# New work lists for the five queues of a sorted-attention and feed-forward kernel, with batch 1's k loaded between the halves of w_in

## The chip, the cores and the metric

The kernel runs on one core of a Trainium2 chip. A core has five instruction queues that run at once: TensorE (PE: matmuls, with the loads of their weights shown as PEld), VectorE (DVE), ScalarE (ACT), GpSimd (POOL) and SyncE (SP), and DMA queues beside them. The metric is device microseconds of one launch; lower is better. All times below are microseconds (us).

## What is computed

Four batches of eight heads, 768 positions and head size 64 go through an attention in which the blocks of k and v are mixed by a matrix that is first balanced by five Sinkhorn rounds; the result is the input of a feed-forward layer. Scale, the subtraction of maxima inside the rounds and the small epsilons are left out here:

```python
P = sort_net                                  # (4, 8, 8, 8)
for _ in range(5):
    P = exp(P - max(P)); P = P / sum(P, -1); P = P / sum(P, -2)
k_sorted = einsum('bhij,bhjcd->bhicd', P, k_blocks)   # 8 blocks of 96 positions
v_sorted = einsum('bhij,bhjcd->bhicd', P, v_blocks)
scores = scale * q_blocks @ k_sorted.T        # block against block, 96 x 96
attn = softmax(scores)
x = (attn @ v_sorted) as (3072 tokens, 512)
h = x @ w_in                                  # (512, 2048)
g = max(h, 0) + alpha * min(h, 0)
out = g @ w_out                               # (2048, 512)
```

## The kernel before

**An order written out by hand.** The body first describes all work as a graph of 1227 numbered operations, each with the engines that may do it, what it reads and writes, and a function that issues its instructions. It then hands `SEQ`, a list of the 1227 numbers, to `G.arrange`. For each engine the operations are issued in the order in which they stand in `SEQ`; a letter behind a number (p, a, d) puts an operation that has a choice on POOL, ACT or DVE, and one without a letter goes to its first engine. `emit` derives the semaphore waits from reads and writes, so any order that `arrange` accepts computes the same. A second table, `WARM`, puts extra matmuls of the identity into PE's queue: `89:14:y` is fourteen of them ahead of operation 89, into the bank `y`. They compute nothing that is used. `BURST` is a count of small matmuls of zeros that PE does first.

**The start (batch 0).** POOL issues the loads: q (op 4), k (5), v (6), batch 1's k (138), w_in in four parts (130 to 133), w_out in two (134, 135), batch 1's v (147, 148) and its q by heads (139 to 146). The Sinkhorn rounds (42 to 78) run on DVE and ACT; a matmul (79) spreads the mixing matrix and DVE makes the block mask BDK (80) from it.

- q is turned in six units: matmuls against the identity (odd ops 81 to 91), each with a copy into QTz on ACT (the even ops behind them, 82 to 92).
- k is mixed and turned in six units (matmuls 93, 95, 98, 100, 102, 104), each with a copy into KT by ACT or DVE (94, 96, 99, 101, 103, 105) and one small copy for a pad of KT (97).
- v is first spread in eight copies (106 to 113, POOL or DVE), then mixed in eight units (matmuls 114 to 128, even), each with a copy into VS by ACT or DVE (115 to 129, odd).

**Attention by groups.** A group is one block of one batch over all eight heads; there are 32, numbered g. For a group PE makes scores (for g = 0 op 149, for g = 1 op 158), DVE their maxima (150, 159), PE the scores once more in the other orientation with the maxima subtracted ("second scores", 151, 160), ACT the exponentials ET (152, 161), PE the product with v (153, 162), DVE the reciprocal of the sums and the scaled result xq (154, 155), PE a transpose (156, 165), and DVE or ACT the copy into xT (157, 166). From batch 1 on, transposes are done by DMAs that SP issues. For g = 2 the scores are 184 and the second scores 186, for g = 3 scores 205, second scores 207, product 209 and transpose 212, for g = 4 scores 238 and second scores 240; these stand among the first feed-forward units.

**Feed-forward.** For two groups at first, later four, sixteen units of w_in: four (or two) matmuls, a relu of the negative on ACT, and a fused multiply and add on DVE that writes hT. The first ones are ops 193 and 196, then 199, 202 and so on. Every 128 tokens follow four quarters against w_out, a copy out of the bank and a store.

**Batches 1 to 3** are prepared between feed-forward units. k and v are spread into zero-padded tiles by POOL or DVE copies ("conv": for batch 1's k ops 247 to 250, 253, 254, 257, 258 and so on; for the first piece of batch 3's v op 713), mixed by PE with the masks BDM and BDV (251 and 255 are the first units of batch 1's k, 252 the copy of the first; the matmuls at line 629 are these units) and copied by ACT or DVE. The masks of batches 1 to 3 come from a second spread (167 to 176). q of batches 1 to 3 is turned by DMA transposes (batch 1's six are 178 to 183); batch 3's v (643 to 646) is loaded when the last q turn of batch 2 (570) has landed. Group 13's scores are op 561, its exponentials 564; op 674 is the feed-forward unit that needs the place they free.

The engines' orders around the change, before, in the numbers above (PE until the first feed-forward, warm-up matmuls as [w]):

```
POOL loads: 4 5 6 138 130 131 132 133 134 147 148 ... 135 ... 139-146
PE: burst [w14] 89 83 81 87 91 85 [w8] 79 [w2] 93 102 [w2] 104 95 100 98 [w9] 114 [w6] 158 118 116 120
    149 124 160 136 122 126 [w4] 128 151 [w1] 162 [w3] 153 177 165 156 184 167 196
```

The rules that fix an operation's engine and a copy's choice are these:

```python
EITHER = ("act", "dve")
SHIFT = ("pool", "dve")
letters = {"p": "pool", "a": "act", "d": "dve"}
e = letters.get(x[-1], op.engs[0])
op.eng, op.pos, op.start = e, len(self.order[e]), float(n)
```

Lines that the profile names: 372 copies by `copy`; 419 and 435 the loads of k and v; 409 the q turns of batches 1 to 3; 539 and 543 the first spread and the mask BDK; 600 the matmuls of `pairs` (q turns and batch 0's k); 629 k of batches 1 to 3; 653 the spread copies of batch 0's v; 669 and 674 the v units; 712, 715, 727, 736 scores; 721 maxima; 759 exponentials; 768 the product with v; 776 and 779 reciprocal and xq; 794 the transpose; 808 warm-up; 823, 833 and 836 the feed-forward's matmuls, relu and fused operation; 862 the second matmuls.

Of the kernel before, what the change touches and what calls it, by code (L numbers as in the profile page):

```python
# [39 lines left out]
155 20 21 165 156 166d 141 184 157a 167 185 140 168 142 169 196 193 186 194 197 195 199 198 187 27 202 170 203 205  # L42
200 204 188 201 214 206 220 215 217 189 218 207 221 219 222 226 216 229 190 227 223 230 273 228 224 171 208 231 225
235 191 236 238 192a 237 232 239 261 313p 251 262 209 233 347p 252a 240 210 263 139 211 255 241 270 234 403 212 264
404 256a 213d 291 301d 271 242 258p 175 259 292 257p 274 260a 352p 265 272 267 311p 243 266 279 244 300p 293 280
268 312p 281 282 269 310p 294 245 174 285 304d 351p 246d 275 286 283 348p 287 284 338 305p 302 339 295 303a 314 288
296 315 306 289 316 340 307a 290 176 297 320 178 341 317 276 318 321 319 179 298 322 379 299a 308 380 323 309a 342
326 324 343 349 344 327 381 350a 325 328 345 353 382 346d 329 354d 332 180 330 572p 383 333 331 357 277a 402 334
335 384 361 360p 385 183 336 373 362 574p 337 358a 363 391p 419 359d 386 355p 364 420 367 573p 365 374 368 366 182
421 356d 388 387d 370 389d 395p 375 577p 369 371 392 390p 435 372 393a 429 394p 436 396 430 376 397d 422 437 445p  # L50
431 432 578p 377d 398 446p 181 453 399d 447p 405 454 449p 438 433 455 465 448p 400 434 459 401a 466 456 460 451 461
457 406 467 452d 483 458 415 423 450d 477 462 478a 475p 468 172 424 413 495 476d 463 407 425 484 378 418 496 408
411 464 481 482a 409d 412 486 485 426 479p 549 487 427d 497 480p 488 439 506p 507 440 492 508d 509p 489 414 441 493
498 511 494 505p 490 442 525 443a 491 510p 516 278 512a 417 526 513 517 535p 537 518 514 469 550 571p 527 515 416
470 519 471 536p 522 538d 520 528 472 561 523 521 539 473a 562 543 540a 499 524 544 541 428 551 500 563 501 546
542d 534 502 545 575 503a 597 576d 547 555 474 548 529 556 606 530 558 607a 612p 557 564 552 609p 531 559 608p 560
610 553a 444 579 613d 638p 611a 598 582 580 532 635 583 637d 591 581 599 636d 585 570 584 592 586 533a 639 600 587
588 640a 626 589 614 627 641 615 565 590 646 593 628 566 644 616 617 643 642d 620 645 567 618 629 594 621 619 622
677 595a 568 504 623 678 569a 659 624 601 410 660 662 602 679 603 554 663 625 661 604 668 605a 718p 680 704 669
713p 671 705 714p 664 672 706 673 665 670 630 719 631 674 666a 632 752p 707 648 686 675 649 633 676 692 687 667  # L60
748p 634a 716d 596 720a 739 688 650 681 689 749d 715p 717d 698 647 690 658 750 691 699 693 751a 700 652 701 173 740
778p 721 702 682 753p 694 703 722 741 723 695 754 724 755d 696a 742 727 683 725 854p 779 726 728 733 777p 729 812p
768 848d 730 654 769 756 731 655 780a 708 732 734 757 709 657 782d 770 783 758 735 813p 784d 651 762 710 771 759
849p 763 656 743 764 760 814 736 847p 711 815a 761 850p 781d 803 744 853p 737d 785 653 684 804 765 786 788 766 805
767 789 787 794 745 797 806 838 798 816 839 772 817a 790 795 799 818 697 840 791 773 796 738 774 820 746 819d 800
792a 775 807 801 851 826 821 802 852a 793 822 873 823 841 874 832 824 881 833 827 747 888p 882a 834 875 828 825 846
808 855 884d 809 885 835 856 883d 685 911p 886a 857 842 887p 836 829 912p 837 712 909 843 830a 861 858 862 910a 901
863 867 859 831 860 889 902 876 913 864 890 891 868 811 865 844 903 869 914d 866 895 915 904 892 896 897 870 893
810 916a 894 877 871a 917 935 776 918 898 936 920 899 919 937 921 900 878 879 929 926 880 961 927 905 962 930 922
938 928 981 963 931 923 906 845 907 932 943 964 933 987 934 944 982 924d 908 988 939 946 945 983 989 940 941 949  # L70
955 947 990 965 948 956 950 1007 958 1008 951 959 1009 960 952 957 972 966 967 969 1010 973 984 974 970 953a 971
872 1033 985a 978 925 1034 975 979 991 980 976 1018 1035 992 977 998 1019 999 1036 995 1000 1020 996 942 997 1004
993 1059 1005 968 1001 1060 1021 1002 1061 954 1003 1047 1006 1011 1015 1024 1016 1048 1017 1025 1012 1026 1085
1027 1022d 1013 1030 1023 1028 1079 1031 1014 1032 1080 1029 994 1044 1086 1041 1045 1062 1081 1046 1042 1087 1043
1049 986 1053 1037 1054 1056 1055 1050 1057 1058 1067 1051d 1105 1068 1038 1070 1039 1116 1071 1040 1072 1117 1069
1088 1076 1106 1073 1077 1063 1078 1074 1082 1075 1096 1064 1083a 1065 1093 1097 1118 1098 1094 1107 1095 1119 1102
# [203 lines left out]
def bass_sinkhorn_attn__then__act_prelu_kernel(  # L280
# [749 lines left out]
```

## Time and profile before

| | us |
|---|---|
| time, median of 3 runs | 238.87 (238.43 to 239.08) |
| the profiled execution's own time | 238.79 |
| its span in the trace | 237.1 |
| PE busy | 228.4 (2511 matmul rows) |
| PE loading weights, beside it | 143.5 |
| DVE busy | 169.4 |
| ACT busy | 151.9 |
| POOL busy | 74.1 |

The profile is of one execution. Its span begins with the first instruction and is 1.7 us shorter than the time of that execution. A row of the timeline has the start, the duration, the engine, the line of the kernel, what is written from what, the shape, how many instructions, and in brackets the idle time before it with what ended it. PE is the engine with the most work; its warm-up matmuls count as busy too, so its share does not say by itself how much of it the computation needs.

### The profile page before, as it was taken

What the parts mean: (1) busy time and instruction counts of PE and PEld (TensorE: products, weight loads), DVE (VectorE), ACT (ScalarE), POOL (GpSimd) and SP (SyncE); (2) the same over time, 40 slices, a digit from 0 to 9 for tenths busy, and PEclk for the clock granted to TensorE, in tenths of its full rate; (3) what the DMA queues carried; (4) which work ended last, traced back from release to release, by engine and by line L of the source; (5) the groups of instructions that cost most, each with busy time, mean ns of one, the idle gap of its engine ahead of it and who ended that gap; (6) DMA issues with size and microseconds to landing.
All of it is one profiled execution on the core that took longest, in us unless ns stands there. A gap on an engine that the chain in (4) does not pass through costs nothing.

```text
span 237.1 us, 6254 instructions
## 1 busy us (share of the span) xinstructions
PE 228.4 (96%) x2511; PEld 143.5 (61%) x2540; DVE 169.4 (71%) x353; ACT 151.9 (64%) x423; POOL 74.1 (31%) x140
## 2 busy tenths in 40 slices
PE   7798999999999999999999999999999999999995
PEld 3455678788666666666566665655655555555544
DVE  4745788889999997878887667676766587744350
ACT  4463356677886988886678786756863646353332
POOL 7959812905759521238292020000000000000000
PEclk9999999999999999999999999999999999999999
DMA  5999999999999998999999795542442423600033
GB/s 93 211 215 170 209 219 200 177 210 156 191 93 150 148 129 176 155 181 179 141 100 131 188 179 119 99 91 48 124 100 74 97 50 82 136 0 0 4 133 133
DMA packets 71453, 31.36 MB, mean 132 GB/s; under 512 B 64504, under 2 KB 65280, under 8 KB 71424
## 3 DMA queue, kind: packets, MB, share of 16 engines
q0 software_dynamic: 22896, 13.63, 44.0%
q1 hardware_dynamic: 48528, 17.33, 38.6%
q8 instruction: 20, 0.33, 0.6%
q14 instruction: 9, 0.07, 0.1%
HBM read 27.28 MB, written 6.29 MB: 142 GB/s over the span
## 4 chain that ended last, share of the span: by engine, by line
PE 90%; DMA 3%; DVE 3%; issue 1%; ACT 1%; POOLq 0%
PE psH L823 34%; PE psYP L862 29%; PE psS L862 4%; PE psS L712 3%; DMA hT<-in_q_dram 3%; PE psO L768 3%; PE psYP L808 3%; PE psYP L669 2%; PE psYP L629 2%; PE psS L727 2%; PE psO L794 1%; PE psS L736 1%; PE psS L715 1%; PE psO L862 1%; DVE hT L836 1%
## 5 line engine op out<-in xcount | busy, mean ns | idle before, releaser
L836 DVE SCALAR_TENSOR_TENSOR hT<-t,omaT,psH 128x384 bf16<-128x384 f32 (+1 forms) x139 | 77.3, 570 | 36.2 <-ACT t L833 34.8
L823 PE MATMUL psH<-xT,w_in_bf 128*128 128x384 bf16 (+1 forms) x556 | 96.9, 311 | 0.1
L833 ACT ACTIVATE t<-psH 128x384 f32<-128x384 f32 (+1 forms) x139 | 63.2, 462 | 49.5 <-PE psH L823 48.2
L862 PE MATMUL psYP<-w_out_bf,hT 128*128 128x512 bf16 x308 | 77.6, 379 | 1.5
L823 PEld LDWEIGHTS psH<-xT,w_in_bf 128*128 128x128 bf16 x556 | 49.5, 98 | 29.1 <-DVE hT L836 1.9
L862 PEld LDWEIGHTS psYP<-w_out_bf,hT 128*128 128x128 bf16 x336 | 30.9, 98 | 28.2
L748 ACT ACTIVATE Esb<-psS,nf 96x96 bf16<-96x96 f32 x192 | 46.3, 346 | 2.0 <-DVE nf L721 2.0
L721 DVE TENSOR_REDUCE nf<-psS 96x8 f32<-96x768 f32 x24 | 22.8, 950 | 6.5 <-PE psS L712 6.0
L658 POOL COPY VDz<-VST 64x192 f32<-64x192 f32 x39 | 20.5, 525 | 20.2 <-DMA VST<-in_v_dram 16.5
L779 DVE TENSOR_TENSOR xq<-psO,rec 96x512 bf16<-96x512 f32 x31 | 21.2, 683 | 0.5
L616 POOL COPY KSz<-KS 64x256 f32<-64x256 f32 x28 | 11.5, 412 | 32.1 <-PE psYP L629 18.8
L401 POOL DMA_DIRECT2D QN<-in_q_dram x24 | 20.0, 839 | 3.3 <-DMA QTz<-QN 2.7
L712 PEld LDWEIGHTS psS<-KT,QTz 128*96 128x96 bf16 x192 | 12.1, 124 | 3.3
L808 PE MATMUL psYP<-identb 128*128 128x512 bf16 x48 | 13.6, 419 | 0.4 <-ACT identb L372 0.4
L372 ACT ACTIVATE VS<-psYP 112x512 bf16<-112x512 f32 x15 | 10.3, 686 | 5.4 <-PE psYP L674 3.2
L768 PEld LDWEIGHTS psO<-VS,ET 112*128 112x128 bf16 x248 | 11.1, 98 | 3.6 <-ACT ET L759 0.2
L768 PE MATMUL psO<-VS,ET 112*128 112x65 bf16 x248 | 12.7, 194 | 0.0
L712 PE MATMUL psS<-KT,QTz 128*96 128x96 bf16 x192 | 12.6, 208 | 0.0
L372 ACT ACTIVATE KT<-psYP 128x512 bf16<-128x512 f32 x15 | 9.0, 599 | 2.6 <-PE psYP L629 1.6
L372 ACT ACTIVATE outstg<-psYP 128x512 f32<-128x512 f32 x13 | 7.7, 604 | 3.2 <-PE psYP L862 3.2
L669 PEld LDWEIGHTS psYP<-BDV,VDz 128*128 128x128 bf16 x192 | 8.2, 98 | 2.3 <-ACT VS L372 0.2
L669 PE MATMUL psYP<-BDV,VDz 128*128 128x64 bf16 x192 | 9.5, 193 | 0.0
(137 smaller groups left out, 200.2 us busy)
## 6 DMA issues: line engine op xcount, KB each, us to landing
out_dram<-outstg SPq DMA_DIRECT2D x23, 256.0 KB, 2.5
KS<-in_k_dram POOLq DMA_DIRECT2D x3, 768.0 KB, 13.6
QN<-in_q_dram POOLq DMA_DIRECT2D x24, 96.0 KB, 5.4
w_in_bf<-in_moe_w_in_dram POOLq DMA_DIRECT2D x4, 512.0 KB, 17.0
w_out_bf<-in_moe_w_out_dram POOLq DMA_DIRECT2D x2, 1024.0 KB, 23.6
VST<-in_v_dram POOLq DMA_DIRECT2D x4, 384.0 KB, 17.9
hT<-in_q_dram POOLq DMA_DIRECT2D x1, 768.0 KB, 7.8
VST<-in_v_dram POOLq DMA_DIRECT2D x1, 768.0 KB, 11.0
```

The costliest lines, as they stand in the source:

```text
L372: return e.activation(o, i, ACTF.Copy) if e is nc.scalar else e.tensor_copy(o, i)
L669: inst = e.matmul(AP(t, off + dd * 64, [[row, 128], [1, 64]]), AP(VDz, (u % VSL * 4 + dd // 2) * 256 + dd % 2, [[VSL * 1024, 128], [2, 128]]),
L712: inst = e.matmul(o, AP(QTz[n], hp * 3072 + h4 * 768 + i * 96, [[6144, 128], [1, 96]]), AP(KT[n], (h4 * 8 + i) * bk, [[ld, 128], [64, 2], ...
L721: G.add(DVE, lambda e: e.tensor_reduce(AP(nx, 0, [[8, 96], [4, 2], [1, 4]]), AP(psX, 0, [[1024, 96], [512, 2], [96, 4], [1, 96]]), AxisLis ...
L748: inst = e.activation(AP(Esb[me], p * 128, [[1024, 96], [64, 2], [1, 48]]), AP(psX, (p // 4) * 512 + (p % 4) * 96, [[1024, 96], [48, 2], [ ...
L768: inst = e.matmul(AP(psZ, hp * 512 + h4 * 68, [[1024, 128], [1, 65]]), AP(ET[me] if far else ET[m], pos(h4, hp) * 96, [[800, nk], [1, 128] ...
L779: G.add(DVE, lambda e: e.tensor_tensor(out=AP(xq[me], 0, [[512, 96], [256, 2], [64, 4], [1, 64]]), in0=AP(psZ, 0, [[1024, 96], [512, 2], [ ...
L808: inst = e.matmul(AP(bank[0], bank[1], [[1024, 128], [1, 512]]), identb[:, :], AP(identb, 0, [[128, 128], [0, 4], [1, 128]]))
L823: inst = e.matmul(AP(pt, poff, [[1024, 128], [1, n]]), AP(w_in_bf, kt * DFF + ft // 2 * 256 + ft % 2, [[KT_TILES * DFF, 128], [2, 128]]), ...
L833: G.add(ACT, lambda e: e.activation(AP(t1[tb], 0, [[384, 128], [1, n]]), AP(pt, poff, [[1024, 128], [1, n]]), ACTF.Relu, scale=-1.0), t_ac ...
L836: G.add(DVE, lambda e: e.scalar_tensor_tensor(out=AP(hT, ft * RING + tok % RING, [[FT_TILES * RING, 128], [1, n]]), in0=AP(t1[tb], 0, [[38 ...
L862: inst = e.matmul(AP(bank[0], bank[1], [[1024, 128], [1, n]]), AP(hT, ft * RING + tok % RING, [[FT_TILES * RING, 128], [1, 128]]), AP(w_ou ...
```

## The change

Three tables change and nothing else: `BURST`, `WARM` and `SEQ`. The first eight entries of the list of operations differ little; from the ninth on all five queues have another order. The count of operations is the same, 1227. 84 of them change their engine: copies that spread v of batches 1 to 3 (13 from POOL to DVE, 7 back), copies that spread k (9 from POOL to DVE, 5 back), the copies behind v units (10 from DVE to ACT, 9 back) and k units (5 and 2), the copies out of the last feed-forward bank (7 from DVE to ACT, 5 back), the xT copies (5 and 5) and two small ones (the clearing of VD0 and KT's pad, from POOL to DVE). DVE has 365 operations instead of 353, POOL 124 instead of 136, ACT 254 as before.

The warm-up table goes from 11 entries with 51 matmuls to 10 with 39, and the burst from 130 to 122 matmuls. The diff, with the long list cut to the part around the start:

```diff
-BURST = 130
+BURST = 122
 WARM = """
-89:14:y 79:8:y 93:2:y 104:2:y 114:9:y 158:6:y 153:3:h 205:1:y 207:1:y 128:4:y 162:1:y
+91:10:y 79:7:y 102:2:y 104:2:y 118:6:y 116:9:y 153:2:h 167:1:p 214:1:y 207:1:y
 """
 SEQ = """
-0 7 11 2 3 1 4 8 42 9 22 28 43 14 44 45 46 47 19 18 48 5 49 50 15 51 39 52 53 6 54 55 25 56 138 57 58 29 23 59 60
-12p 61 62 130 63 64 31 65 32 66 13 37 89 67 68 83 69 81 84 70 87 71 91 131 88 10 85 132 72 40 73 90 133 74 75 86
-134 76 41 77 82 78 26 79 92 147 80 148 93 102 94d 103a 104 95 105a 100 98 99a 38 109d 106p 35 111d 36 96a 108p 112d
-16 34 101a 33 114 107p 115d 97p 146 158 118 159 110p 116 119a 120 250p 149 121d 124 248p 160 117d 125a 113p 30 135
-136 161 122 137 150 249p 126 254p 127a 123d 24 128 144 151 129d 143 247d 17 152 162 145 163 164 153 177 253p 154
...
+0 7 11 2 27 3 10 1 4 42 43 8 9 91 28 44 40 45 46 47 48 49 50 51 52 53 54 55 56 57 39 81 85 87 89 83 5 24 20 6 130
+26 131 138 132 133 134 147 25 13 23 148 146 135 19 16 58 59 60 61 62 63 64 65 66 67 86 68 69 70 71 72 29 37 82 38
+73 74 35 75 76 77 78 79 80 102 93 103d 94a 84 88 14 247p 253p 250p 21 144 143 249p 145 141 140 15 254p 31 248p 98
+12d 104 95 100 41 108d 111d 34 17 110d 92 99a 105a 90 96a 109d 97d 101d 118 113d 112d 107d 106d 116 114 158 119d
+149 124 159 115a 120 150 121d 160 125a 117a 122 136 123d 161 126 128 129a 151 152 36 137 127d 33 162 163 164 153
...
```

In the new order POOL's loads are 4, 5, 6, 130, 131, 138, 132, 133, 134, 147, 148, 146, 135, then 144, 143, 145, 141, 140 with copies of batch 1's k between them (247, 253, 250 ahead of 144). PE's start reads: burst, [w10], 91 81 85 87 89 83, [w7] 79, [w2] 102 93 98, [w2] 104 95 100, [w6] 118, [w9] 116 114 158 149 124 120 160 122 136 126 128 151 162, [w2] 153 177 165 184 156, [w1] 167 193 196.

More of the change, by code (lines that the diff above doesn't have):

```diff
@@ L45 @@
[L45 to L64, printed above, removed]
@@ new lines @@
+229 239 236 230 240 225 237 210 231 232 241 211 251 261 252d 273 262 233 263 212 291 213a 234 292 255 270 256a 264
+242 259 293 271 265 260a 294 272 173 266 243 244 279 313p 257p 258p 301p 30 310p 300p 311p 351p 267 282 268 274 280
+269 283 302 281 284 338 303a 245 285 339 305p 22 142 139 32 403 348p 347p 352p 312p 246a 288 306 286 295 289 304d
+287 290 296 297 340 307a 314 315 317 275 308 318 341 316 319 320 323 321 298 324 309d 379 349 322 299a 325 326 350a
+380 329 342 327 353 330 178 381 354a 343 328 332 357 179 333 331 335 344 358d 276 345 388 336 382 337 180 364 334
@@ new lines @@
+389d 419 359p 356p 390p 355p 404 394p 402 360p 391p 346a 365 277a 361 392 383 362 420 366 384 385 363 373 370 374
+421 393d 371 372 386 367 422 387a 368 435 396 432 397a 369 433 429 430 375 436 437 434 18 398 456 395d 431 399d 457
+458 453 400 376 454 450p 446p 578d 462 465 447p 577p 449p 448p 455 172 445d 466 377a 401a 463 459 460 405 423 451
+406 464 461 424 452d 425 467 181 183 278 438 182 468 378 483 495 477 496 486 426 484 478a 427d 485 487 497 407 481
+439 489 488 492 490 475p 574p 506p 505p 479p 510p 476p 440 571d 441 572p 415 413 418 480p 408 442 525 491 493 482a
@@ new lines @@
+443a 409a 494 526 513 469 514 470 471 507 516 549 515 508d 472 519 527 517 498 528 511 520 550 512a 473d 499 518
+522 523 521 500 501 176 524 537 538a 561 543 502 562 411 535p 412 536p 509p 414 417 416 544 503a 545 539 546 547
+563 551 529 555 564 556 548 530 531 540d 573d 558 557 559 560 552 597 541 532 579 553a 542a 582 580 533d 598 581
+583 428 570 599 591 575 565 585 584 588 566 576d 606 608d 592 593 626 600 589 607a 610 567 590 586 613d 609d 587
+611a 646 612p 644 637p 643 645 617 618 627 638d 614 615 619 568 594 635 628 569d 616 601 623 620 595d 602 636d 662
@@ new lines @@
+765 735 814 815d 762 766 763 767 764 803 736 794 737a 785 795 786 804 816 788 796 743 800 787 817d 744 745 805 789
+797 838 771 684 711 801 798 818 772 819a 802 849d 823 790 839 840 847p 854d 791 773 799 848d 851 774 792a 820 873
+824 826 821 852a 853d 874 825 822 875 746 806 775 841 876 697 827 881 807 882a 808 809 828 832 835 885 842 829 833
+834 836 837 830d 653 884p 685 712 747 888p 887p 912p 883p 911p 886a 855 843 844 856 909 858 901 867 910a 859 857
+860 902 913 861 862 914d 864 868 915 863 916d 903 865 877 889 890 869 935 870 891 878 866 871a 936 895 892 896 893
@@ new lines @@
+904 738 937 897 894 879 880 810 938 793 920 921 917 898 961 905 922 923 899 918 900 919 906 962 907 926 929 924a
+927 930 963 908 845 964 776 811 831 872 949 981 928 931 939 943 932 944 945 987 940 950 955 933 934 956 946 947 982
+951 988 957 941 989 969 948 970 971 958 1007 952 975 965 959 960 972 1008 953a 976 973 974 977 966 983 1018 978 995
+1009 1033 984 979 996 985a 980 998 999 1034 997 1019 1001 1000 967 1035 1004 990 942 991 1047 1020 1002 1003 1015
+1059 1010 954 846 925 1005 1006 992 993 1024 1011 1021 1048 1016 1025 1060 1017 1026 1022d 1012 1013 1061 1030 1036
@@ new lines @@
+968 1023 986 1014 994 1062 1027 1031 1032 1079 1085 1044 1028 1029 1045 1041 1049 1080 1086 1042 1046 1056 1087
+1043 1057 1058 1053 1054 1050 1037 1055 1038 1039 1051a 1070 1067 1105 1081 1071 1072 1076 1068 1069 1077 1073 1063
+1116 1106 1078 1096 1074 1064 1075 1065 1097 1098 1093 1088 1082 1089 1102 1094 1095 1103 1099 1100 1090 1083d 1091
+1101 1104 1107 1137 1117 1113 1122 1118 1119 1114 1123 1124 1128 1115 1120a 1129 1130 1125 1126 1066 1052 1108 1092
+1040 1084 1109 1161 1138 1110 1127 1111 1131 1134 1139 1162 1112 1132 1135 1133 1136 1146 1147 1143 1144 1145 1148
@@ L83 @@
+1140 1163 1149 1152 1141a 1150 1153 1182 1164 1151 1154 1158 1159 1160 1165a 1155 1183 1170 1203 1156 1157 1171
+1172 1167 1184 1176 1168 1169 1177 1178 1185 1173 1209 1188 1174 1175 1179 1204 1221 1189 1190 1194 1180 1186a 1181
+1195 1196 1191 1222 1210 1200 1192 1193 1201 1202 1197 1198 1199 1121 1166 1187 1142 1205 1211 1206 1207a 1208 1212
+1213d 1214 1223 1224 1225 1226 1215 1216 1217 1218 1219 1220
 """.split()
```

28 lines of the change are left out of this document (7 added, 21 removed).

## The prediction, made before the changed kernel was run

> **What bounds the kernel now.** I read the table of stages first, then the chain of waits, then the timeline of the first 31 us.
>
> ```profile
> core 0: us, PE busy (x) PEld busy (x) DVE busy (x) ACT busy (x) POOL busy (x), PEclk, DMA share, GB/s
> 0.00:9.00 9.00, 5.99 (x144) 2.81 (x144) 4.99 (x28) 3.24 (x8) 7.43 (x20) 1.00 0.71 133
> 9.00:18.00 9.00, 8.60 (x220) 5.36 (x221) 5.24 (x22) 6.15 (x15) 6.52 (x10) 1.00 1.04 213
> 18.00:31.00 13.00, 12.11 (x242) 8.10 (x241) 8.09 (x17) 4.48 (x7) 11.45 (x21) 1.00 1.07 193
> 31.00:46.00 15.00, 14.87 (x231) 12.24 (x231) 13.47 (x38) 9.57 (x25) 5.69 (x12) 1.00 1.31 202
> 46.00:100.00 54.00, 53.44 (x659) 36.99 (x666) 48.73 (x95) 44.98 (x131) 25.46 (x47) 1.00 1.20 156
> ...
> PE 90%; DMA 3%; DVE 3%; issue 1%; ACT 1%; POOLq 0%
> ...
> 30.77 0.83 PE L823 MATMUL psH<-xT,w_in_bf 128*128 128x192 bf16 x8
> ```
>
> After 31 us PE is busy 14.87 of 15 us, 53.44 of 54, and so on, and 90% of the chain is PE. All matmuls of the reference are in both lists, so from the first feed-forward matmul (30.77) the rest takes what it takes: a new order can only lose there. What can be won lies before 30.77, where PE's "busy" is partly warm-up, and in what PE waits for.
>
> ```profile
> 9.14 0.44 PE L600 MATMUL psS<-identb,hT 64*64 64x64 bf16 x16 [1.58 <-DMA hT<-in_q_dram]
> ...
> 13.05 0.29 DVE L543 TENSOR_TENSOR BDK<-mkh,psYP 128x128 bf16<-128x128 f32 x1 [0.46 <-PE psYP L539]
> ...
> 16.50 0.34 DVE L653 COPY hT<-VST 128x192 f32<-128x192 f32 x1 [1.85 <-DMA VST<-in_v_dram]
> ...
> 17.71 0.58 ACT L372 ACTIVATE KT<-psO 128x512 bf16<-128x512 f32 x1
> ...
> 20.53 0.95 DVE L721 TENSOR_REDUCE nm<-psH 96x8 bf16<-96x768 f32 x1 [1.01 <-PE psH L715]
> ...
> 16.07 0.28 PE L600 MATMUL psO<-BDK,KS 64*64 64x64 bf16 x6 [0.26 <-issue]
> ...
> 23.45 0.46 PE L727 MATMUL psH<-identb,nm 96*112 96x96 bf16 x6 [0.77 <-issue]
> ...
> 23.95 0.81 ACT L759 ACTIVATE ET<-psH 112x768 bf16<-112x768 f32 x1 [1.11 <-PE psH L727]
> ...
> 25.24 0.68 DVE L372 CAST VS<-psO 112x512 bf16<-112x512 f32 x1
> ...
> 26.47 0.70 DVE L372 CAST VS<-psO 112x512 bf16<-112x512 f32 x1 [0.55 <-PE psO L674]
> ...
> 27.45 0.42 PE L768 MATMUL psYP<-VS,ET 112*128 112x65 bf16 x8
> ...
> 16.07:23.45 7.38, 6.61 (x127) 4.02 (x127) 4.40 (x11) 3.29 (x7) 6.35 (x13) 1.00 1.01 180
> ...
> q8 instruction: 20, 0.33, 0.6%
> ```
>
> Batch 0's q lands at 9.1, v at 16.5. Between, the masks (13.05) give K; after v come the spread copies, V and the first two groups; the output of group 1 (op 162) starts at 27.45. Twice PE stops for nothing the profile names ("issue"): at 16.07 and, inside group 1's second scores (op 160), for 0.77 us at 23.45. The two stops are 127 matmuls and 127 weight loads apart, and PE's 5051 instructions divided by the 20 packets of the queue called instruction are 253 each: I read both stops as waits for PE's next block of program. Counting back 128 matmuls from 16.07 gives the last q turn at about 10.4, so a block came 5.65 us and 7.38 us after PE entered the one before it.
>
> **The change, part by part.** Tile code, loads and arithmetic stay; the order of five queues, some engines, 12 warm-up matmuls (51 to 39) and 8 of the burst go.
>
> **Loads.** DMA share is 1.04 from 9 to 18 us, so sending v at about 3.6 instead of 5.47 moves bytes up a queue that is full. I take v's landing as it was; at most it gains those 1.9 us, at least nothing. k of batch 1 goes behind two parts of w_in.
>
> ```profile
> 5.47 0.54 POOL L419 DMA_DIRECT2D VST<-in_v_dram  x1
> ...
> L419 POOL DMA_DIRECT2D KS<-in_k_dram x1: 548/548/548, 6.2 to 6.2; - x1
> DMA to landing us min/median/max: 13.9/13.9/13.9
> ```
>
> Issued at 6.2, it landed 13.9 later, at 20.1. Two 512 KB parts (beside its 768 KB, at 213 GB/s 2.5 us each) put it near 26. POOL then stands at conv_k 247 until 26, and q loads 144, 143, 145, 141, 140 stand behind it. Nothing early needs them: all eight copies of v are now DVE's, and batch 1's first K (251) comes near 38. Cover 3 us; cost nothing, or what passes 3 us.
>
> **To the second scores.** ACT keeps the same spacing, 0.48 (11.21, 11.69 in the next rows). After the masks it has eight copies, op 94 to op 96 of its list, from 14.1 (the mask ends at 13.34, then one unit's matmuls of 0.44 and two semaphores): the last ends at 14.1 + 7 x 0.48 + 0.6, about 18.1, as now (17.71 + 0.58). DVE from 16.5: four spread copies at 0.29 each (two took 0.58 in 16.87 to 17.45), a mask, then KT's pad at 18.1, one KT copy and one V copy (0.62 each) and the other four copies: the max of group 1 starts at about 21.1, against 20.53, so 0.6 later. But op 160 then runs at 22.1 to 22.9 unbroken, because 26 instructions fewer stand before it (13 matmuls with their loads): the block's edge moves from the third matmul of L727 to the ninth of the V unit that follows (op 122). ET of group 1 follows at 23.05 instead of 23.95.
>
> **The block's edge in op 122.** PE enters the block before it at about 17.45 (op 118, behind six warm-ups). With 5.65 and 7.38 the next comes at 23.1 or 24.85; I take the middle, 24.0. Op 122 could start at 23.05, so PE waits there 0.7 us (0 to 1.6). From the copy of that unit to the end of the last V copy the old chain took 26.47 + 0.70 - 25.24 = 1.93; op 122's rest and a semaphore 0.25, and 0.1 to op 162: 26.3. That is 1.15 earlier than 27.45.
>
> **To the first feed-forward.** Now 30.77 - 27.45 = 3.32. In the new list both xT copies are ACT's, one 0.48 behind the other, with fewer warm-ups between: I take 3.45. First feed-forward at 29.75, **1.0 us earlier** (0.15 to 1.7 by the two block times).
>
> **31 to 46 us.** DVE was busy 13.47 of 15 here, and the new list gives it one K copy more (252) and takes an xT copy away.
>
> ```profile
> 11.21 0.57 ACT L372 ACTIVATE QTz<-psS 128x512 bf16<-128x512 f32 x1
> 11.69 0.57 ACT L372 ACTIVATE QTz<-psO 128x512 bf16<-128x512 f32 x1
> ...
> 33.91 0.41 DVE L836 SCALAR_TENSOR_TENSOR hT<-t,omaT,psYP 128x192 bf16<-128x192 f32 x1
> ...
> 34.24 0.94 DVE L721 TENSOR_REDUCE nm<-psS 96x8 bf16<-96x768 f32 x1
> ...
> 35.11 0.19 DVE L776 RECIPROCAL rec<-psO 96x8 f32<-96x8 f32 x1
> ...
> 36.48 0.68 DVE L779 TENSOR_TENSOR xq<-psO,rec 96x512 bf16<-96x512 f32 x1
> ...
> 37.08 0.40 DVE L836 SCALAR_TENSOR_TENSOR hT<-t,omaT,psYP 128x192 bf16<-128x192 f32 x1
> ...
> 40.89 0.40 PE L629 MATMUL psYP<-BDM,KSz 128*128 128x64 bf16 x8
> ```
>
> Spacings: hT 0.33, max 0.87, xq 0.60. From the first feed-forward: max of group 3 at 3.1; then hT, rec, hT, xq, a mask and three hT (0.33 + 0.12 + 0.33 + 0.60 + 0.15 + 1.0) and ACT's ET between bring the max of group 4 to 6.8, its second scores to 8.0, and PE to op 212 at 10.5. The old list has the same matmuls done at 40.89 - 30.77 = 10.1. **Loss 0.4** (0 to 0.8). The 4 us after that hold: PE's work outweighs DVE's.
>
> **After 46 us** I count nothing; that is bounded by the rivals. The last ten PE operations are the same, so the tail is too.
>
> Sum: 1.0 - 0.4 = 0.6 us off the profiled execution's 238.79 (span 237.1, 1.7 around it), which stands 0.08 below the median of 238.87. Predicted **238.3**, inside the 0.3% (0.72 us) that a measurement of this kernel can hardly tell from no change.
>
> **Rivals.**
>
> *The block comes when it is asked for.* With 23.1 op 162 starts at 25.6 and the first feed-forward at 29.05: 1.7 gained, and if DVE's list costs only 0.2, 1.5: **237.4**. For it: 5.65 was seen. Against: 7.38 was seen under the same DMA share, and later.
>
> *The block comes late.* With 24.85: 0.15 gained, 0.4 lost: **239.1**.
>
> *PE's clock falls.* Ten warm-ups before q instead of 14: by the next rows they end about 6.7, and PE stands until 9.1, 2.4 us; now 1.58.
>
> ```profile
> 2.81 4.75 PE L808 MATMUL psYP<-identb 128*128 128x512 bf16 x14 [0.38 <-ACT identb L372]
> ...
> 4.91 0.15 PEld L808 LDWEIGHTS psYP<-identb 128*128 128x128 bf16 x1 [0.28 <-issue]
> ...
> 5.34 0.15 PEld L808 LDWEIGHTS psYP<-identb 128*128 128x128 bf16 x1 [0.28 <-issue]
> ...
> 6.10 0.96 PEld L808 LDWEIGHTS psYP<-identb 128*128 128x128 bf16 x5 [0.18 <-issue]
> ```
>
> The loads come 0.43 apart until about 6, then 0.19: half clock, then full. If a stand of 2.4 us throws it back, six q turns (1.5 us) and seven warm-ups (1.5) double, and the mask matmul waits for them until 15 instead of 12.6. ACT's eight copies move by 2.4; DVE can do v's copies meanwhile, so some 1.4 of it stays: **239.7**. The trace has no stand between 1.58 and 2.4. The Trainium skill, "TensorE: Matmul & The Clock Gate", Part 1 (the HAM clock gate), says that the clock falls after a whole idle window of about 3.4 us, which 2.4 cannot fill; by that rule the sum stays 238.3. The trace agrees for what it shows: 1.58 did not throw it.
>
> *A load comes late into DVE's queue (the other side).* Batch 3's v is loaded after a q turn has landed. Its first copy is now at the head of DVE (op 713), before three feed-forward halves; it was POOL's.
>
> ```profile
> L435 POOL DMA_DIRECT2D VST<-in_v_dram x4: 535/539/547, 94.0 to 95.6; - x4
> DMA to landing us min/median/max: 3.6/4.6/6.9
> ...
> L409 SPq DMA_TRANSPOSE QTz<-QN x5: 1231/1265/1392, 82.7 to 90.7; - x5
> DMA to landing us min/median/max: 3.1/4.1/5.1
> ```
>
> From the scores of group 13 (561) to the matmul that needs that place (674) PE has 14 feed-forward units of 0.65, 8 quarters of 0.86 and small ones for 5.3: 21.3 us. The chain beside it: scores and max 2.3, wait and exponentials 3.0, two transposes issued 2.5, landing 4.1 to 5.1, three issues and two copies on POOL 2.4, last piece 3.6 to 6.9, copy and hT 1.1: 19.0 to 23.3. It decides from 21.3; at its worst 2.0 us: **240.3**.
>
> **Chances.** Forecast 0.43 (237.8 to 238.8: faster 0.16, same 0.26, slower 0.01); early block 0.22; late block 0.15 (same 0.11, slower 0.04); clock 0.07 (slower 0.06); late load or another late wait after 46 us 0.13. Faster 0.38, same 0.38, slower 0.24. Left out at each end about a tenth: 236.9 (v earlier as well) to 240.1.
>
> **What would show it.** Right: v's first copy at 16.5, op 160 unbroken, a stop by "issue" in op 122 near 23.3 to 24, first feed-forward at 29.0 to 30.6, PE some 0.4 us behind by 46, nothing after. Wrong: q turns 0.5 us apart, v landing earlier, DVE waiting for VST near 102, PE idle over 0.1 us in 10 after 46.

## The result, and the profile after

The changed kernel takes 244.88 us (median of 4, 244.59 to 248.05); the kernel before took 238.65 beside it (237.97 to 239.08). The ratio is 1.0294, with a 95% interval from 1.0252 to 1.0337: slower by some 6 us, far outside the range that was forecast. The ratios, here and in the table of the experiments, leave out executions more than 1.5% above the fastest of their kernel, while the medians are of all, so a ratio need not be the quotient of the two medians beside it. The profiled execution took 244.59, with a span of 242.9.

The table of stages of the changed kernel, as before with two rows more (columns: stretch, its length, busy us of each engine, granted clock, DMA share, GB/s):

```profile
9.00:18.00 9.00, 8.90 (x215) 5.73 (x216) 4.97 (x22) 4.35 (x11) 5.09 (x8) 0.81 1.01 183
...
31.00:46.00 15.00, 14.92 (x237) 12.18 (x237) 13.02 (x33) 10.30 (x27) 8.41 (x18) 1.00 1.30 202
46.00:100.00 54.00, 54.00 (x654) 37.13 (x654) 48.30 (x98) 45.17 (x131) 26.75 (x49) 1.00 1.12 144
100.00:116.00 16.00, 16.00 (x164) 9.96 (x163) 13.69 (x28) 12.45 (x39) 4.86 (x9) 1.00 1.11 163
116.00:130.00 14.00, 9.89 (x75) 5.56 (x73) 7.66 (x14) 5.26 (x15) 8.78 (x13) 0.88 1.45 157
```

The same stretch of the kernel before:

```profile
116.00:130.00 14.00, 13.89 (x145) 8.69 (x143) 11.48 (x21) 9.80 (x29) 8.14 (x14) 1.00 1.56 103
```

Read PE's busy time (the second number) and its clock (third from the end). Up to 116 us PE is never short of work. From 116 to 130 it stands for 4.1 of 14 us, and its clock is 0.88, which is 14 x 0.12 = 1.7 us of lost pace; it issues 75 matmuls where it issued 145. That is 5.8 us, as much as the spans differ (242.9 - 237.1). Two more views name the waits: the chain's shares, where DMA went from 3% to 9%, and PE's waits after 46 us (line waited for, us in sum, times, longest), of which the kernel before has none.

```profile
PE 84%; DMA 9%; DVE 2%; ACT 2%; issue 1%; SPq 0%; DVEq 0%; POOLq 0%
```

```profile
PE psYP L669 <- issue: 2.3, 1, 2.3
PE psO L768 <- DMA ET<-Esb: 2.0, 2, 1.8
```

The timeline around that place shows where they come from:

```profile
105.56 1.21 SPq L753 DMA_TRANSPOSE ET<-Esb  x1
106.81 1.14 SPq L876 DMA_DIRECT2D out_dram<-outstg  x2
...
108.00 1.81 SPq L409 DMA_TRANSPOSE QTz<-QN  x1
108.08 1.07 POOL L419 DMA_DIRECT2D KS<-in_k_dram  x2 [2.10 <-DVE xT L372]
...
110.62 3.11 SPq L753 DMA_TRANSPOSE ET<-Esb  x1
...
118.14 5.01 POOL L401 DMA_DIRECT2D QN<-in_q_dram  x6 [9.00 <-DMA QTz<-QN]
...
120.43 0.43 PE L768 MATMUL psO<-VS,ET 112*128 112x65 bf16 x8 [1.78 <-DMA ET<-Esb]
...
124.39 1.07 POOL L658 COPY VDz<-VST 64x192 f32<-64x192 f32 x2
...
125.56 0.58 PE L669 MATMUL psYP<-BDV,VDz 128*128 128x64 bf16 x8 [2.32 <-issue]
```

Follow it from the end. PE's unit at 125.56 is op 814 (batch 3's v, unit 5). It needs op 778, the second copy of the pair at 124.39 on POOL. The profile names no releaser for the stop of 2.32 ("issue"); that it is this copy is shown by moving the copy, below. POOL is late because it first issues six loads of batch 3's q (5.01 us of issue), then makes one copy and issues a seventh load, and before all that stands for 9.00 us: those loads overwrite QN, and the last q turn of batch 2 (op 534) must have read it. That turn is the SP row at 108.00, issued behind group 16's transpose (680) and two stores. In the kernel before it was the second of three turns from 82.74 on; op 534 went out at 84.1. POOL there had only two of the q loads ahead of the pair with op 778:

```profile
82.74 4.05 SPq L409 DMA_TRANSPOSE QTz<-QN  x3
...
110.23 1.67 POOL L401 DMA_DIRECT2D QN<-in_q_dram  x2
...
111.94 1.10 POOL L658 COPY VDz<-VST 64x192 f32<-64x192 f32 x2
```

The view of that one instruction in the changed kernel (who waited for it, and its time to landing):

```profile
  POOL QN L401: 9.0, 1
...
DMA to landing us min/median/max: 9.6/9.6/9.6
```

Group 17's ET (the SP row at 110.62, op 707) takes 9.8 to land as well, which is PE's other wait, 1.78 at 120.43. Behind these two stands PE's clock is half from 125.6 to 129.0. In the start it falls too:

```profile
2.80 3.95 PE L808 MATMUL psYP<-identb 128*128 128x512 bf16 x10 [0.42 <-ACT identb L372]
...
9.03 0.44 PE L600 MATMUL psS<-identb,hT 64*64 64x64 bf16 x16 [2.28 <-DMA hT<-in_q_dram]
...
16.52 0.50 DVE L653 COPY hT<-VST 128x192 f32<-128x192 f32 x2 [0.17 <-DMA VST<-in_v_dram]
...
24.10 0.45 PE L674 MATMUL psO<-BDK,hT 128*64 128x64 bf16 x16
...
30.19 0.83 PE L823 MATMUL psH<-xT,w_in_bf 128*128 128x192 bf16 x8
```

The clock of two short stretches of the same execution:

```profile
10.00:12.00 2.00, 2.00 (x58) 1.64 (x55) 1.00 (x6) 1.69 (x5) 1.94 (x4) 0.50 0.97 200
126.00:129.00 3.00, 3.00 (x18) 1.66 (x16) 2.23 (x4) 0.49 (x1) 1.15 (x2) 0.50 1.26 106
```

The first feed-forward starts at 30.19 instead of 30.77. Counting the matmul work done up to each row of PE, the changed kernel is 0.6 us ahead at 30 us, 0.2 at 46, 0.9 at 116, then 5.1 behind at 129 and 5.8 at the end. The 0.7 between 129 and the end is lost near 160; by what is open.

### The profile page after: what moved, and what is told of

It reads as the page before. It is cut to its first block, busy times and chain, and to the rows that moved or that the text cites. A ratio compares the mean times of both kernels' runs of the same rounds, so it can differ in the third digit from the quotient of the medians.

```text
span 242.9 us, 6243 instructions
## 1 busy us (share of the span) xinstructions
PE 231.5 (95%) x2522; PEld 144.3 (59%) x2522; DVE 170.6 (70%) x365; ACT 152.7 (63%) x423; POOL 68.4 (28%) x128
## 4 chain that ended last, share of the span: by engine, by line
PE 84%; DMA 9%; DVE 2%; ACT 2%; issue 1%; SPq 0%; DVEq 0%; POOLq 0%
PE psH L823 31%; PE psYP L862 27%; DMA ET<-Esb 4%; PE psS L862 4%; PE psS L712 3%; DMA hT<-in_q_dram 3%; PE psO L768 3%; PE psYP L808 3%; PE psYP L669 2%; PE psYP L629 2%; DMA xT<-xq 2%; PE psS L727 2%; PE psO L794 1%; PE psS L736 1%; PE psS L715 1%
## 5 line engine op out<-in xcount | busy, mean ns | idle before, releaser
L823 PE MATMUL psH<-xT,w_in_bf 128*128 128x384 bf16 (+1 forms) x556 | 97.9, 312 | 0.1
L862 PE MATMUL psYP<-w_out_bf,hT 128*128 128x512 bf16 x336 | 83.7, 381 | 0.0
L616 POOL COPY KSz<-KS 64x256 f32<-64x256 f32 x24 | 9.7, 405 | 28.3 <-PE psYP L629 15.1
L372 ACT ACTIVATE outstg<-psYP 128x512 f32<-128x512 f32 x16 | 9.5, 595 | 8.7 <-PE psYP L862 8.7
L768 PEld LDWEIGHTS psO<-VS,ET 112*128 112x128 bf16 x248 | 10.6, 98 | 5.8 <-DMA ET<-Esb 1.9
L712 PE MATMUL psS<-KT,QTz 128*96 128x96 bf16 x192 | 12.9, 211 | 0.0
L808 PE MATMUL psYP<-identb 128*128 128x512 bf16 x39 | 12.3, 452 | 0.4 <-ACT identb L372 0.4
L372 DVE CAST VS<-psYP 112x512 bf16<-112x512 f32 x12 | 8.2, 682 | 4.3 <-PE psYP L669 4.3
L372 ACT ACTIVATE VS<-psYP 112x512 bf16<-112x512 f32 x14 | 9.6, 684 | 0.8 <-PE psYP L669 0.2
## 6 DMA issues: line engine op xcount, KB each, us to landing
KS<-in_k_dram POOLq DMA_DIRECT2D x3, 768.0 KB, 10.3
```

The lines of the kernel that those rows point to most:

```text
L372: return e.activation(o, i, ACTF.Copy) if e is nc.scalar else e.tensor_copy(o, i)
L712: inst = e.matmul(o, AP(QTz[n], hp * 3072 + h4 * 768 + i * 96, [[6144, 128], [1, 96]]), AP(KT[n], (h4 * 8 + i) * bk, [[ld, 128], [64, 2], ...
L768: inst = e.matmul(AP(psZ, hp * 512 + h4 * 68, [[1024, 128], [1, 65]]), AP(ET[me] if far else ET[m], pos(h4, hp) * 96, [[800, nk], [1, 128] ...
L823: inst = e.matmul(AP(pt, poff, [[1024, 128], [1, n]]), AP(w_in_bf, kt * DFF + ft // 2 * 256 + ft % 2, [[KT_TILES * DFF, 128], [2, 128]]), ...
L862: inst = e.matmul(AP(bank[0], bank[1], [[1024, 128], [1, n]]), AP(hT, ft * RING + tok % RING, [[FT_TILES * RING, 128], [1, 128]]), AP(w_ou ...
```

## The experiments

Theory T: op 534 is late, and POOL, standing for it, holds the copies that PE needs. Rival R: the new order crowds transfers together, and they are late whatever the order. Each kernel was timed beside the kernel before on its own chip; the ratio is to that one.

| kernel | median us | before, same chip | ratio (95%) |
|---|---|---|---|
| changed | 244.88 | 238.65 | 1.0294 (1.0252 to 1.0337) |
| e1_turn_early | 238.64 | 238.09 | 1.0000 (0.9952 to 1.0049) |
| e2_pool_first | 240.85 | 238.09 | 1.0084 (1.0027 to 1.0141) |
| e3_warm14 | 245.33 | 238.09 | 1.0208 (1.0127 to 1.0290) |
| e4_hybrid | 248.37 | 238.09 | 1.0248 (1.0162 to 1.0335) |
| e5_before_late | 238.51 | 240.36 | 0.9970 (0.9932 to 1.0008) |
| e6_stores_late | 239.67 | 240.36 | 0.9988 (0.9946 to 1.0030) |
| e7_all | 245.27 | 240.36 | 1.0247 (1.0200 to 1.0295) |
| e8_early_warm14 | 239.14 | 240.36 | 0.9959 (0.9926 to 0.9992) |
| f1_before_warm18 | 239.20 | 239.71 | 1.0001 (0.9965 to 1.0038) |
| f4_before_warm10 | 238.49 | 239.71 | 0.9967 (0.9931 to 1.0002) |
| f2_early_stores_warm18 | 239.05 | 239.71 | 0.9993 (0.9961 to 1.0026) |
| f3_loads_behind | 239.64 | 239.71 | 1.0015 (0.9982 to 1.0047) |
| g1_before_all_three | 243.38 | 238.84 | 1.0196 (1.0148 to 1.0244) |
| g2_before_late_loads | 239.06 | 238.84 | 1.0030 (0.9995 to 1.0064) |
| g3_changed_again | 245.58 | 238.84 | 1.0194 (1.0124 to 1.0265) |

### One operation moved: the turn early

```diff
- 444 504 474 704 705 680 ... 740 741 534 707 742
+ 444 504 474 534 704 705 680 ... 740 741 707 742
```

> The changed kernel with one operation moved: the q turn 534 (batch 2, piece 4) stands on SP right behind turn 474, ahead of group 16's transpose (680), instead of behind it and two stores. Theory T (a late turn blocks POOL): POOL's stand of 9.0 us ahead of batch 3's q loads shrinks to under 3 us, the 2.3 us stop of PE ahead of op 814 and the half clock behind it (1.5 us) go, and group 17's ET (op 707) has one transfer less in front: 238.9 to 241.0. Rival R (crowded transfers): from 108 to 118 us every transfer takes 7 to 10 us whatever the order, so PE still waits 1.8 us for group 17's ET and POOL still stands over 5 us: 243.5 to 245.

Its ratio is 1.0000, as fast as the kernel before; one of its four executions took 243.19 and was not profiled. In its timeline POOL doesn't stand for a turn any more; the six loads go out at 108.57, 9.6 us earlier than in the changed kernel:

```profile
108.57 4.93 POOL L401 DMA_DIRECT2D QN<-in_q_dram  x6 [0.23 <-issue]
...
111.36 0.42 PE L768 MATMUL psO<-VS,ET 112*128 112x65 bf16 x8 [1.44 <-DMA ET<-Esb]
```

Moving one operation of 1227 takes the loss away. Transfers around it still take 7 to 10 us (group 17's ET: 9.8), so R alone does not make it. One wait of 1.44 for group 16's ET is left.

### The copies ahead of the loads

```diff
- 647 658 652 654 655 657 651 813p 656 ... 784a 770 781p 778p 709
+ 647 778p 781p 813p 658 652 654 655 657 651 656 ... 784a 770 709
```

> The changed kernel with three copies of batch 3's v (ops 778, 781, 813) moved on POOL ahead of the q loads that stand for the turn; the turn stays late. Theory T: the 2.3 us stop ahead of op 814 and the half clock behind it (1.5 us) go, the 1.8 us wait for group 17's ET stays: 240.6 to 241.4. Rival R: the crowd of transfers is the cause, not POOL's order, and the next late thing takes the place of the stop: 243.5 to 245.

240.85, as T had it. POOL's and PE's waits from the views of waits:

```profile
POOL QN L401 <- DMA QTz<-QN: 6.0, 1, 6.0
```

```profile
PE psO L768 <- DMA ET<-Esb: 2.0, 1, 2.0
```

The turn still lands late and POOL still stands, but PE's stop ahead of op 814 is gone; the wait for group 17's ET remains, and the clock falls behind it (0.61 from 121 to 124). So the copies' place on POOL is a link of the chain, and the late ET is a second wait of its own.

### The stores out of the way

```diff
- 741 534 707 742 ... 596 ... 667 ... 554
+ 741 534 707 742 667 596 554
```

> The changed kernel with three stores of results (554, 596, 667; 256 KB each) moved on SP behind group 18's transpose (742); the turn 534 stays behind 680. Theory T+R (the turn is late because it stands in SP's queue behind a crowd of four stores and four loads of k; take 768 KB out of the crowd and it lands 2 to 4 us earlier): POOL's stand 9.0 falls to 4 to 6 us, the wait for group 17's ET goes, 240 to 242. Theory T alone (only its place behind 680 counts): the turn lands as late as before, 244 to 245.

239.67, a little better than T+R had it. The turn goes out at 107.7 as in the changed kernel, but it lands after 6.1 instead of 9.6:

```profile
  POOL QN L401: 5.0, 1
...
DMA to landing us min/median/max: 6.1/6.1/6.1
```

```profile
PE psYP L669 <- issue: 0.3, 1, 0.3
```

3.5 us at the turn take 2.0 off the stop and the whole wait for group 17's ET. So T alone falls: what is in flight beside the turn (in the changed kernel four stores of 256 KB and four loads of 192 KB within 9 us) is part of the cause. Two things stay open. Three of the ten executions took 244.4 to 245.4, as long as the changed kernel, and none of these was profiled. And the turn now goes out 0.63 us ahead of the next load of k, where it was 0.08 (108.00 and 108.08):

```profile
107.72 1.52 SPq L409 DMA_TRANSPOSE QTz<-QN  x1
...
108.35 1.06 POOL L419 DMA_DIRECT2D KS<-in_k_dram  x2 [2.10 <-DVE xT L372]
```

A load issued on top of the turn is therefore a rival for these 3.5 us, and no experiment separates the two: the turn took 8.1 to 10.7 to land in the four executions with that load at most 0.1 us behind it (changed, e2, e3, g3). The stores do count by themselves, though: group 17's ET goes out 0.05 us behind a load of q in e1, e8, f2 and f3 alike, and lands after 9.8 and 8.9 with three stores just ahead of it (e1, e8), after 6.2 and 6.5 with one (f2, f3).

### The late turn put into the kernel before

```diff
- 428 ... 534 502 545 ... 474 ... 680 ... 707 648
+ 428 ... 502 545 ... 474 ... 680 ... 707 534 648
```

> The kernel before with one operation moved the other way: the q turn 534 stands on SP behind group 17's transpose (707) instead of 25 us earlier. Theory T (a late turn on SP blocks POOL, which blocks copies that PE needs): the turn lands at 113 to 117, POOL stands 3 to 7 us at op 658, the copies behind it are late by as much and PE loses 1.5 to 5 us: 239.6 to 243. Rival R (only the crowd of transfers that the new list makes): no more than 0.5 us: 238.0 to 238.7.

A miss for T as I had put it: no loss. POOL does stand, for 3.6 us, but in that list only two of the q loads stand ahead of the copies, and PE never waits. So I changed the theory: it takes three things together, a late turn, a crowd that delays its landing, and six loads ahead of the copies. Two kernels put two and all three into the kernel before:

```diff
- 680 ... 707 ... 667 ... 658 652 778p 753p ... 654 655 657 ... 651
+ 680 554 410 ... 707 667 534 ... 658 652 654 655 657 651 778p 753p
```

> The kernel before with the three ingredients put in: the q turn 534 on SP behind group 17's transpose (707) and a store (667); stores 554 and 410 behind 680, so that four stores and four loads of k are in flight with it; and on POOL six q loads (658, 652, 654, 655, 657, 651) ahead of the copies 778 and 753, where two were. Theory T3 (all three together make the loss, each alone is covered): the turn lands at 115 to 118.5, POOL stands 4 to 7 us, the loads take 5.0 more, copy 753 ends at 121 to 124 and PE, which wants op 783 at 119.7, waits 1.5 to 4.5, with half a clock behind it (1.5) where it waits over 2: 240.5 to 244.5. Rival (the new list has another weakness that these edits don't carry): 238.0 to 239.5.

> The kernel before with two of the three: turn 534 behind 707, and six q loads ahead of the copies 778 and 753; the stores stay where they were. Theory T3: the turn lands near 114, the loads end near 119, copy 753 near 120.3 and op 783 waits 0.3 to 1: 238.4 to 239.6. Rival (the order on POOL alone makes the loss): 241 and more.

g2, without the stores, is within 0.64% of the kernel before; g1 is 1.96% slower. POOL's timeline in g1, and the unit that waits:

```profile
115.15 4.93 POOL L401 DMA_DIRECT2D QN<-in_q_dram  x6 [5.37 <-DMA QTz<-QN]
...
120.12 1.08 POOL L658 COPY VDz<-VST 64x192 f32<-64x192 f32 x2
...
121.35 0.58 PE L669 MATMUL psYP<-BDV,VDz 128*128 128x64 bf16 x8 [1.99 <-POOL VDz L658]
```

In g2 the turn landed after 5.6 and POOL stood for 3.3; in g1, with the stores, after 7.0 (here too the next load of k moved, from 1.22 us behind the turn to 0.59). The 2 us more that POOL stands in g1 are past what PE has in hand, and the clock falls again (0.56 from 121 to 124). g1 has the stand of the copies, not the wait for group 17's ET, and it shows some 4.5 us of the 6.

> The changed kernel itself, unaltered, on the same chip as the two others, for a second profiled execution. Theory T3: the same places as in the first (POOL standing for a q turn near 110 to 118, PE waiting for group 17's ET and ahead of op 814): 243.5 to 246, 5 to 7 above the kernel before. Rival (the first profile showed an accident): PE's waits between 116 and 130 us under 1 us in sum, and the loss elsewhere.

The second profiled execution loses at the same places: POOL stands 8.5 for the turn, PE waits 1.4 for group 17's ET and 2.0 ahead of op 814:

```profile
119.69 5.00 POOL L401 DMA_DIRECT2D QN<-in_q_dram  x6 [8.51 <-DMA QTz<-QN]
...
127.09 0.39 PE L669 MATMUL psYP<-BDV,VDz 128*128 128x64 bf16 x8 [1.96 <-issue]
```

The first profile was no accident. The single times go from 241.9 to 246.65.

### The clock at the start

```diff
-91:10:y 79:7:y
+91:14:y 79:7:y
```

> The changed kernel with 14 warm-up matmuls instead of 10 ahead of the q turns, as before; nothing else. Theory S1 (the half clock from 9.6 to 13.0 us is hidden behind v's landing and DVE's copies): first feed-forward within 0.2 us of 30.19, time within 0.3 us of the changed kernel (244.6 to 245.2). Theory S2 (it is on the path): q turns 0.26 apart, first feed-forward 0.5 to 1.1 us earlier, time 243.8 to 244.4.

The time can't tell, since the places above and one at 55.8 us (1.5 for a q turn of batch 1) cover it; the timeline can: the q turns run at full rate and the first feed-forward starts 1.8 us earlier, part of it because q landed earlier in this execution.

```profile
8.67 0.44 PE L600 MATMUL psS<-identb,hT 64*64 64x64 bf16 x16 [0.78 <-DMA hT<-in_q_dram]
...
28.39 0.83 PE L823 MATMUL psH<-xT,w_in_bf 128*128 128x192 bf16 x8
```

The same count was then changed in the kernel before, to 10 and to 18:

> The kernel before with 10 warm-up matmuls instead of 14. Theory K: warm-ups end near 6.8, the stand is 1.9 to 2.9 us, the clock falls in nearly every execution (mean 0.993), q turns 0.43 apart, first feed-forward at 32.2 to 32.6, time 239.8 to 240.8. Rival (the half clock is hidden here): time 238.0 to 238.8 with a mean clock of 0.993.

> The kernel before with 18 warm-up matmuls ahead of the first q turn instead of 14. Theory K (PE standing more than about 1.9 us for q throws its clock to half for 3.4 us, and that is worth about 1.7 us at the end): the warm-ups end near 8.5, the stand is under 1 us, mean clock 1.0 in every execution, 238.0 to 238.8 in all of them; faster than the kernel before only by the share of its executions that fall. Rival: mean clocks of 0.993 stay as frequent as in the kernel before; then the cause lies elsewhere.

With 10 the clock fell (first fence), with 18 it didn't (second); q landed at the same time in both:

```profile
8.95 0.47 PE L600 MATMUL psS<-identb,hT 64*64 64x64 bf16 x10 [2.56 <-DMA hT<-in_q_dram]
...
30.46 0.83 PE L823 MATMUL psH<-xT,w_in_bf 128*128 128x192 bf16 x8
```

```profile
8.95 0.44 PE L600 MATMUL psS<-identb,hT 64*64 64x64 bf16 x16 [0.46 <-DMA hT<-in_q_dram]
...
30.75 0.83 PE L823 MATMUL psH<-xT,w_in_bf 128*128 128x192 bf16 x8
```

Theory K fell: in the kernel before a half clock here is worth nothing (30.46 against 30.75), and both times are those of the kernel before. In the changed list it is worth about 1.0: with 18 warm-ups (f2) q landed at 9.04 and the first feed-forward came at 29.20, against 9.03 and 30.19.

```profile
9.04 0.44 PE L600 MATMUL psS<-identb,hT 64*64 64x64 bf16 x16 [0.68 <-DMA hT<-in_q_dram]
...
29.20 0.83 PE L823 MATMUL psH<-xT,w_in_bf 128*128 128x192 bf16 x8
```

Where then do the kernel before's own executions of 239.6 to 241 with a mean clock of 0.993 come from? One execution of that kind is profiled, that of e5 (240.44), whose start is the kernel before's:

```profile
24.00 0.66 PE L727 MATMUL psH<-identb,nm 96*112 96x96 bf16 x6 [1.33 <-issue]
...
32.43 0.75 PE L823 MATMUL psH<-xT,w_in_bf 128*128 128x192 bf16 x7
```

```profile
24.00:27.00 3.00, 3.00 (x43) 2.16 (x43) 1.64 (x3) 1.50 (x2) 2.68 (x4) 0.52 1.12 209
```

It is the stop that the prediction put down to a late block of program: 1.33 us here instead of 0.77. Behind it the clock is half from 24.1 to 27.5, and the first feed-forward is 1.66 later than 30.77.

### Hybrids and repairs

> The changed kernel's order up to its op 646 (about 93 us, with its burst and warm-up tables), then all remaining operations in the order and on the engines of the kernel before. Theory T (all the loss is made behind 108 us by the new order, what comes before is a gain of about 1.0 us): 237.2 to 238.2. Rival R (the new order's earlier part leaves transfers crowded, or the seam makes a wait of its own): 239 to 241.

The changed list up to op 646, then the old one: 242.89 to 254.34, worst of all. Its profiled execution (250.97) is among the long ones; it shows a place that the changed kernel has too, but did not pay for in its profile:

```profile
74.93 0.87 PE L712 MATMUL psS<-KT,QTz 128*96 128x96 bf16 x8 [8.81 <-DMA QTz<-QN]
```

```profile
68.00:74.00 6.00, 0.00 (x0) 0.00 (x0) 1.04 (x3) 0.36 (x1) 0.00 (x0) 0.79 1.30 27
```

A q turn of batch 1 (180, issued at 53.18) landed after 21.7 us; batch 2's k (404) had been issued 0.2 us behind it. The queues were busy all the time (share 1.30) and moved 27 GB/s. Its shorter executions (242.89 and 245.77) were not profiled.

> The changed kernel with four edits: 14 warm-ups ahead of q; turn 534 behind 474; batch 2's k load (404) on POOL right behind 403, ahead of batch 1's q turns, instead of on top of them; stores 410 and 554 right behind group 14's transpose (600) on SP instead of inside the crowd behind 680. If the causes are right (clock, late turn, crowds near 55 and 108 us), all of the early gain of about 2 us stays: 235.8 to 237.0, below the kernel before. Rival: the order has a next weak place, or the loads moved to 48 us delay batch 1's turns: 237.5 to 240.

The rival's mechanism held, and cost more: with op 404 at 48.8, ahead of the turns, turns 178 and 179 took 8.9 and 10.3 to land and PE waited 4.7 for the first of them, until 60.32. Moving this load earlier was wrong.

> The changed kernel with two edits: 14 warm-ups ahead of q and turn 534 behind 474. Against the same kernel with four edits this tells what the two crowds cost. If crowds cost much and in some executions only: median 237.5 to 239 with single times of 240 and more. If they cost nothing: the same as with four edits, 236 to 237.

> The changed kernel with 18 warm-ups ahead of q, the turn 534 behind 474, and stores 554, 596, 667 behind 742. If the three causes (clock at the start, late turn, crowd near 108 us) are all, it stays 0.5 to 2 us below the kernel before: 236.5 to 238.3. Rival: batch 1's q turns, which land by the load queue and not by PE, take back what the start gains: 238.3 to 239.3.

> The same as the kernel with three edits, and batch 2's loads 404 and 402 on POOL behind two more copies (360, 391), so that they are issued behind the third q turn of batch 1 (180) and not on top of it. Theory C (a load issued on top of a transpose makes it land 10 to 22 us later instead of 4 to 5): turn 180 lands within 7 us, no single time above 241, median 0 to 1 us below the kernel with three edits. Rival: the collision only moves to the next turns (181, 183): no gain.

e8 and f2 are at the kernel before, not clearly below it: 0.9959 (0.9926 to 0.9992) on a chip where 14 of the kernel before's 29 executions had a mean clock of 0.993 or less, 0.9993 on another. In f3 turn 180 landed after 4.1 instead of 10.5 in f2, as theory C had it, but the median did not improve (239.64 against 239.05): the next two turns (181 and 183) took 9.6 and 7.0 where they had taken 6.9 and 4.3, which is the rival. No version was found that clearly beats the kernel before.

## Why the prediction was wrong

**What bounds it, and the loads: right.** v's first copy started at 16.52 (forecast 16.5), k of batch 1 landed at 26.35 (forecast near 26). POOL stood for it, as forecast, and PE did not wait.

**The second scores and the block's edge: the place right, the size not.** Op 160 ran unbroken, and PE's stop is tied to a place in its program: with 14 warm-ups ahead of q it comes behind the fifth matmul of op 122 (e8), with 18 behind the first (f2), four earlier for four more, which puts it at the ninth for ten, as counted:

```profile
22.80 0.38 PE L674 MATMUL psO<-BDK,hT 128*64 128x64 bf16 x11 [0.28 <-issue]
```

```profile
23.12 0.44 PE L674 MATMUL psO<-BDK,hT 128*64 128x64 bf16 x15 [0.24 <-issue]
```

But the term of 0.7 us (0 to 1.6) was too large: in the changed kernel op 122 started at 24.10 with no stop, and no profiled execution of this list shows more than 0.3. (Its table `WARM` holds 41 matmuls, not 39; the 13 fewer ahead of op 160, 5 of them and 8 of the burst, are counted rightly.) The first feed-forward came at 30.19 against 29.75. That it lies between 29.0 and 30.6 is luck: no stop at the edge gained part of what the clock then lost, and where the clock held all through the start (e2, e3, e4, e7, f2) it came at 28.2 to 29.2, nearer to the early-block rival's 29.05.

**The clock: the rival that I gave 0.07 happened.** A stand of 2.28 threw it. It cost the first feed-forward 1.0 (f2) to 1.3 (e7, 28.89, with q landing at 9.06), where I had put 1.4. The rule of the Trainium skill, "TensorE: Matmul & The Clock Gate", Part 1 (the HAM clock gate), that the clock falls after a whole idle window of about 3.4 us, does not agree: 2.28, and in e5 1.33, were enough, and the measurement decides. The half clock then lasted from 9.5 to 12.9, which agrees with a window of that length.

**31 to 46 us: right.** Forecast 0.4 lost; counted by work done, the lead went from 0.6 to 0.2.

**"After 46 us I count nothing": this step failed.** Up to 116 us nothing was lost (the lead even grew from 0.2 to 0.9); behind it 6.7 were. The reason I gave was that PE is busy there all the time in the old list; that says nothing of what the new order makes late. I followed one moved operation, op 713 on DVE, and did name the right kind of mechanism, a load behind a q turn, but on the wrong queue, at 240.3; there DVE stood 1.0 for VST at 100.5 and PE lost nothing. SP's list was not compared line by line. It would have shown a turn moved from 84 to 108 us, past four ET transposes and two stores, and POOL's list behind it shows the six loads and the copies. The sum that was missing is the turn's issue and landing, then 0.5 to the first load, then the 7.4 of loads and copies on POOL (118.14 to 125.56), against the moment at which PE asks for op 814 (123.24, or 121.5 without the wait of 1.78). My estimate of it with the landings in the kernel before, 3.1 to 7.2 for a turn: 108.0 + 3.1 to 7.2 + 7.9 is 119.0 to 123.1, a loss of 0 to 1.6. So the comparison would have named the place, but not the size: that came from landings of 9.6 and 9.8, longer than that of any transpose in the trace of before (7.2 at most), and from the half clock.

**The rivals' chances.** Late load or other late wait after 46 us had 0.13, and its price of 2.0 us was a bound from one chain. Two waits (1.8 and 2.3) and the half clock behind them (1.7) were 5.8; the list of rivals had a late wait and the half clock only one at a time.

## What to carry to other kernels

When all orders change, compare each queue's list with the old one for the operations that others wait for, the DMA issues on SP and POOL first: note what each was moved past, and add up what is queued behind it on every engine that waits. A late transfer is harmless until the sum of its landing, the issues behind it and the copies behind those passes what the bounding engine has in hand, and then each microsecond counts, with the clock on top. Judge such a list by several executions: e6 was as fast as the kernel before in seven of ten and some 5 us slower in three.

## What the hardware showed that was not expected

A transpose by DMA took 3.1 to 5.1 us to land with little beside it (before, the five turns from 82.7 on). Turn 534 took 8.1 to 10.7 in the crowd, with a load of k at most 0.1 us behind it (changed, e2, e3, g3), and 6.1 and 7.0 with that load 0.6 behind it (e6, g1). Turn 180 took 10.2 to 21.7 where batch 2's load of k was issued within 0.7 us of it (e1, e2, e3, e4, e8, f2), and 4.1 to 4.9 where that load came 1.1 us or more behind it (changed, e6, f3, g3). That the queues moved only 27 GB/s then (e4) is shown, why is open.

PE's clock fell behind stands of 1.33 (e5), 1.97 (e2), 1.99 (g1), 2.17 (e6, for q), 2.28 (changed), 2.56 (f4), 2.71 (e1) and 3.01 (g3), and behind one of 0.28 among small matmuls (e8, from 24 on), but not behind 1.58 (before), 1.91 (e3, until 124.6) or 2.09 (e7, for q): the length alone does not decide it. Within one execution the changes of the granted clock lie whole multiples of 3.41 us apart (changed: half from 9.53 to 12.94 and from 125.58 to 128.99, and 125.58 - 12.94 is 33 x 3.41), and in the 3.41 us ahead of a fall PE had mostly been busy for less than half: 0.29 to 0.45 of them ahead of nine of the 13 falls, nothing ahead of two. The stand of 2.09 in e7 lies across such a point (8.24), and PE was busy for 0.63 and 0.76 of the two stretches beside it. It is no sharp rule: 0.61 (e5) and 0.86 (e8) were followed by a fall, 0.43 (e4) and 0.44 (e3) were not.
